# Yields, copy engines, mark times and list limit of a fused FFT and balanced-expert kernel

## The chip, the cores and the metric

The kernel runs on one core of one Trainium2 chip. The metric is the device time of one execution in microseconds (us). Before the change it is 576.92 us, the median of three runs (576.12 to 579.05).

The engines are named as in the profile: PE is TensorE's matmul, PEld its weight load, DVE is VectorE, ACT is ScalarE, POOL is GpSimd, and SP is the engine that issues plain DMAs.

## The reference

The input x has 8 batches of 2496 rows of 256 values. The reference takes the real part of the two-dimensional FFT of each batch, calls the 19968 resulting rows tokens, and gives every token to one of 8 experts, each of which takes exactly 2496 tokens. Then each token goes through its expert's two matrices.

```python
X = np.fft.fft(np.fft.fft(x, axis=1), axis=2).real          # 8 x 2496 x 256
logits = tokens @ w_gate                                    # 19968 x 8
for idx in np.argsort(-logits.flatten()):                   # best pair first
    tok, e = idx // 8, idx % 8
    if assigned[tok] >= 0 or counts[e] >= 2496: continue
    assigned[tok] = e; counts[e] += 1
out[mask_e] = np.maximum(tokens[mask_e] @ w1[e], 0) @ w2[e] # 256 -> 1024 -> 256
```

## The kernel before, in words

**Stages.** Loading, folding by symmetry and cosine/sine tables take the first 80 us or so. Then the logits are computed ahead of the transform. From about 100 us the transform runs in 20 parts (n = 0 to 19) of 1024 token places each. Each part has an even half and an odd half: ten matmuls each into one PSUM tile `fftps` (`even_half`, `odd_half`). ACT scales the even sum into `ev` (L1051) and casts the whole sum into `stage` (L1058). Then the part's *combination* (`combine` inside `odd_half`) writes the difference `ev - fftps` on DVE (L1061), negated columns on ACT (L1062) and mirrored columns on POOL (L1064, L1065), and SP stores 512 KB to `t_dram` (L1067). The combination on DVE is what frees the PSUM tile for a later even half: six of the eight parts that matter here rotate through three buffers "h", every fourth part has one buffer "t". Between the halves stand 16 pieces `wps` (L1104) that fold the feature transform into w1; their PSUM tile is the single buffer "o", which ACT copies out (L1030).

**The first chain.** Beside the transform a chain on DVE (`first_chain`: `choose`, `lowest`, `search`, `first_strips`) finds which tokens surely keep their first choice and gives each a place `spot` in a *strip*. It is a Python generator: a `yield` of some number of microseconds lets the loop `for c in first_chain()` (just before the sort loop) record that many microseconds' worth of transform halves, `unit()`, on the other engines' streams; a `yield SYNC` aligns the two estimated clocks. Every engine's stream is in the order in which it is recorded (a manual schedule), so a yield decides which combinations stand between two steps of the chain on DVE. In `first_strips` three additions of PSUM results (L884: experts 0-2 from a tile "o", 3-5 from "misc", 6-7 from "o" again) are followed by the tree of maxima `top_of` (L595 to L597), ten small operations up to `spot` (L902), the marks of part 0 (`sort_mark(0)`) and one yield of 7.0.

**The first sort.** A sort turns a part's 1024 token rows into rows grouped by expert. `sort_mark(n)` makes eight one-hot tiles `pt` on DVE (L1123, two buffers), `reload(n)` brings the part back from `t_dram` as `xl` (three buffers, L1132), `sort_call(n, gs)` multiplies the two on PE (L1145) and `take` copies PSUM to the strip `xs`. For strip 0 (parts 0 to 3) the PSUM tile alternates between the two single buffers "misc" and "o" (`side_ps`), and both are copied by ACT (L1030). `strip_places` (L911 to L917) and `payloads(0, ...)` (L584 to L589) prepare the row numbers, `sort_rows(0, 0)` (L1158 to L1162) and `sort_rows(0, 1)` (L1172 to L1179) make them; the matmuls of the latter write the PSUM buffer "t", which the combination of part 19 frees.

**The experts.** 40 strip tiles of 384 tokens come first (5 strips by 8 experts), then 16 late tiles: per expert one of 384 and one of LCAP - 384 places, which are gathered by an indirect DMA. Each tile has three parts: 3, 3 and 2 of its eight up products (L1282, ReLU copies by ACT L1030 or DVE L1034), each followed by one down product (L1305) of the tile before, whose 128 rows are copied and scattered to the output by an indirect DMA on POOL (L1309). A table `aside` puts other steps in front of a (tile, part): the marks, sorts and reloads of strips 1 to 4. After each part `pace` lets a second DVE chain, `settle_rest`, go on; it ends with the lists of late tokens (`decode`, L810 to L826), and only then can the gathers of late tiles (L1263, on POOL) be issued. A flag tells whether an expert has more late tokens than LCAP; if so, a slow fallback recomputes everything not placed.

Of the kernel before, what the change touches and what calls it, by code (L numbers as in the profile page):

```python
# [19 lines left out]
S = 2496  # L20
D = 256
# [23 lines left out]
TT = 384  # L45
SEG = 4096
LB = 6
LCAP = 736
SW = 24
NT = 5  # L50
GT = 16
EW = E * SW
# [18 lines left out]
def kernel(  # L71
# [437 lines left out]
    deep = {"ps": None, "sb": None, "n": 0}  # L509
# [84 lines left out]
    def top_of(dst, src):  # L594
        nc.vector.tensor_tensor(tree, src[:, 0:4, :], src[:, 4:8, :], op=AL.max)  # L595
        nc.vector.tensor_tensor(tree[:, 0:2, :], tree[:, 0:2, :], tree[:, 2:4, :], op=AL.max)
        nc.vector.tensor_tensor(dst, tree[:, 0, :], tree[:, 1, :], op=AL.max)  # L597
# [253 lines left out]
    def first_strips():  # L851
        low, wid, lo0 = found["low"], found["wid"], found["lo0"]
        lev = small("lev")
        nc.vector.scalar_tensor_tensor(lev, in0=wid, scalar=-0.01, in1=low, op0=AL.mult, op1=AL.add)
        moved = small("moved")
        nc.vector.tensor_tensor(moved, low, lo0, op=AL.is_gt)
        nc.vector.tensor_scalar(moved, in0=moved, scalar1=2.0 * T_FREE, scalar2=-T_FREE, op0=AL.mult, op1=AL.add)
        fits = small("fits")
        nc.vector.tensor_scalar(fits, in0=exc, scalar1=0.5, scalar2=2.0 * T_FREE, op0=AL.is_lt, op1=AL.mult)
        nc.vector.tensor_scalar(fits, in0=fits, scalar1=-T_FREE, scalar2=None, op0=AL.add)  # L860
        nc.vector.scalar_tensor_tensor(lev, in0=lev, scalar=moved, in1=fits, op0=AL.min, op1=AL.max)
        yield 0.8
        yield SYNC
        bps = misc()
        nc.tensor.transpose(bps[:, 0:P], lev.to_broadcast([P, P]), identf)
        thr = small("thr")
        nc.vector.tensor_reduce(thr, bps[:, 0:P], axis=AXX, op=AL.min)
        nc.vector.tensor_scalar(sure, in0=mx, scalar1=thr, scalar2=0.0, op0=AL.add, op1=AL.is_ge)
        nc.vector.scalar_tensor_tensor(sure, in0=mv, scalar=0.0, in1=sure, op0=AL.is_le, op1=AL.mult)
        nc.vector.scalar_tensor_tensor(ohb, in0=off, scalar=0.0, in1=sure[:, None, :].to_broadcast([P, E, GC]),  # L870
                                       op0=AL.is_le, op1=AL.mult)
        yield 2.3
        yield SYNC
        v = asg.tile([P, GC], FT, tag="sl_v", bufs=1, name="sl_v")
        for e0, ne in ((0, 3), (3, 3), (6, 2)):
            rps = (misc() if e0 == 3 else pso.tile([P, 512], FT, tag="o", bufs=1, name="rps"))[:, 0:ne * GC]
            rv, ov = (v_.rearrange("p (f k) -> p f k", k=NK) for v_ in
                      (rps, ohb[:, e0:e0 + ne, :].rearrange("p e c -> p (e c)")))
            nc.tensor.matmul(rv[:, :, 0:NK:2], lhsT=rankb, rhs=ov[:, :, 0:NK:2], start=True, stop=False)
            nc.tensor.matmul(rv[:, :, 1:NK:2], lhsT=rankf, rhs=ov[:, :, 1:NK:2], start=False, stop=False)  # L880
            nc.tensor.matmul(rps.rearrange("p (f s k) -> p f s k", s=2, k=NK)[:, :, 1, :], lhsT=onesb,
                             rhs=ohb[:, e0:e0 + ne, :].rearrange("p e (f s k) -> p (e f) s k", s=2, k=NK)[:, :, 0, :],
                             start=False, stop=True)
            nc.vector.tensor_tensor(wa[:, e0:e0 + ne, :].rearrange("p e c -> p (e c)"), rps,  # L884
                                    base[:, e0:e0 + ne, :].rearrange("p e c -> p (e c)"), op=AL.add)
        top_of(v, wa)
        v_i = asg.tile([P, GC], I32, tag="sl_vi", bufs=1, name="sl_vi")
        for cc in range(2):
            nc.vector.tensor_scalar(by_cols(v_i, cc), in0=by_cols(v, cc), scalar1=2.0 * SEG - (SW - SC[cc]) - MARK,
                                    scalar2=0.0, op0=AL.add, op1=AL.max)  # L890
        t1 = asg.tile([P, GC], I32, tag="sl_t1", bufs=1, name="sl_t1")
        t2 = asg.tile([P, GC], I32, tag="sl_t2", bufs=1, name="sl_t2")
        t3 = asg.tile([P, GC], I32, tag="sl_t3", bufs=1, name="sl_t3")
        nc.vector.tensor_scalar(t1, in0=v_i, scalar1=13, scalar2=None, op0=AL.arith_shift_right)
        nc.vector.tensor_scalar(t3, in0=v_i, scalar1=SEG - 1, scalar2=None, op0=AL.bitwise_and)
        has = asg.tile([P, GC], FT, name="has_e")
        for cc in range(2):
            hc, sc, vc, a1, a3 = (by_cols(t, cc) for t in (has, spot, v, t1, t3))
            nc.vector.scalar_tensor_tensor(hc, in0=a3, scalar=float(SC[cc]), in1=by_cols(sure, cc), op0=AL.is_lt,
                                           op1=AL.mult)  # L900
            nc.vector.scalar_tensor_tensor(vc, in0=a1, scalar=float(SC[cc]), in1=a3, op0=AL.mult, op1=AL.add)
            nc.vector.scalar_tensor_tensor(sc, in0=vc, scalar=1.0 - SC[cc], in1=hc, op0=AL.add, op1=AL.mult)  # L902
        early["has"] = has
        sort_mark(0)
        yield 7.0
        early["t"] = (v, t1, t2, t3)

    def strip_places():
# [114 lines left out]
    def take(dst, src, relu=False, eng=None):  # L1023
        n = 1
        for d in src.shape[1:]:
            n *= d
        ca, cd = 0.17 + n / 1280.0, 0.13 + n / 900.0
        if eng == "A" or eng is None and busy["A"] + ca <= busy["D"] + cd:
            busy["A"] += ca
            nc.scalar.activation(dst, src, ACT.Relu if relu else ACT.Copy)  # L1030
        else:
            busy["D"] += cd
            if relu:
                nc.vector.tensor_scalar(dst, in0=src, scalar1=0.0, scalar2=None, op0=AL.max)  # L1034
            else:
                nc.vector.tensor_copy(dst, src)  # L1036
# [81 lines left out]
    def sort_mark(n):  # L1118
        marks[n] = moe.tile([P, 8, EW + 2], BF, tag="pt", bufs=2, name="pt")
        b0, kc = NB * (n // NK), n % NK  # L1120
        for f in range(8):
            c, w = b0 * 4 * NK + f * NK + kc, E * SC[f % 2] + 1
            nc.vector.tensor_scalar(marks[n][:, f, 0:w], in0=rampw[:, 0:w], scalar1=spot[:, c:c + 1],  # L1123
                                    scalar2=None, op0=AL.is_equal)
        busy["D"] += 1.1
# [8 lines left out]
    def sort_call(n, gs, eng=None):  # L1134
        t, u = divmod(n, 4)
        if t not in strips:
            strips[t] = (deep["sb"] if t % 2 else moe).tile([P, 2, E, SW // 8, GT, 8], BF, tag="xs", bufs=1, name="xs")
        xl, pt = reloads[n], marks[n]
        dst = strips[t].rearrange("p j e c g i -> p (j e c) g i")
        for g in gs:  # L1140
            sps = side_ps("sps", eng)
            for cc in range(2):
                for j2 in range(2):
                    into = sps[:, j2 * EW:(j2 + 1) * EW].rearrange("p (e s) -> p e s", s=SW)
                    nc.tensor.matmul(into[:, :, SW - SC[cc]:], lhsT=xl[:, 2 * g + cc, j2 * P:(j2 + 1) * P],  # L1145
                                     rhs=pt[:, 2 * g + cc, 0:E * SC[cc]].rearrange("p (e s) -> p e s", s=SC[cc]), start=(cc == 0 and j2 == 0),
                                     stop=(cc == 1 and j2 == 1))
            take(dst[:, :, 4 * u + g, :], sps[:, 0:2 * EW].rearrange("p (m i) -> p m i", i=8), eng=eng)

    def sort_rows(t, part):  # L1150
        a_t = a8
# [47 lines left out]
    for c in first_chain():  # L1199
# [7 lines left out]
        clock["D"] = max(clock["D"], clock["PE"]) + 0.3  # L1207
        clock["PE"] = max(clock["D"], clock["PE"])
    for n in range(4):
        if n < 3:  # L1210
            sort_mark(n + 1)
        unit()
        sort_call(n, (0, 1), "A")
        unit()
        sort_call(n, (2, 3), "A")
        unit()
        reload(n + 3)
        if n == 0:
            strip_places()
        if n == 1:  # L1220
            payloads(0, payr)
    sort_rows(0, 0)
    while unit():
        pass
    flush()
# [121 lines left out]
    for t in range(1, NT):  # L1347
        for u in range(4):
            j, n = 8 * (t - 1) + 2 * u, 4 * t + u
            at(j, 0, lambda n=n: sort_mark(n))  # L1350
            at(j, 2, lambda n=n: sort_call(n, (0, 1)))
            at(j + 1, 1, lambda n=n: sort_call(n, (2, 3)))
            if n + 3 < 4 * NT:
                at(j + 1, 2, lambda n=n: reload(n + 3))
        at(8 * t - 4, 1, lambda t=t: sort_rows(t, 0))
        at(8 * t - 1, 0, lambda t=t: sort_rows(t, 1))
# [102 lines left out]
```

## Time and profile before

| | us |
|---|---|
| median of three runs | 576.92 |
| the profiled execution's own time | 526.67 |
| its span, first to last instruction | 524.8 |
| PE, PEld, DVE, ACT, POOL busy | 463.1, 349.5, 359.3, 331.9, 333.6 |

The profiled execution is 50.25 us faster than the median of the runs. Busy times are those of the span. In a timeline each row gives the start, the duration, the engine, the source line, the operation with its output and input tiles and the number of merged instructions; in brackets stands how long the engine sat idle before the row and what ended the wait. In a table of windows each row is a stretch of the span with the busy time of PE, PEld, DVE, ACT and POOL, then TensorE's granted clock as a share of full speed, the busy share of the DMA engines and what they moved in GB/s.

### The profile page before, as it was taken

Reading aid. Unit: us, or ns where it says so; the run is one execution under the profiler, and the core shown is the slowest. Engines: PE = TensorE matmul, PEld = TensorE weight load, DVE = VectorE, ACT = ScalarE, POOL = GpSimd, SP = SyncE. Lnnn points to the kernel's source line nnn. Section 1 sums busy time; section 2 is a strip of 40 time slices with the busy share of each in tenths; the row PEclk is TensorE's granted clock in tenths of the full one; section 3 lists DMA queues with packets and bytes.
Section 4 is the critical chain, followed back from the end, with each engine's and each line's share of the span. In section 5 each row is a group of like instructions: output and inputs, shape, how many; then the busy total and the mean of one; then the engine's idle time right before and its main releaser. Section 6 shows DMA issues by size and latency. Waiting matters only on the chain. (4 is left out here: it accounts for less than half of the span.)

```text
span 524.8 us, 11144 instructions
## 1 busy us (share of the span) xinstructions
PE 463.1 (88%) x3943; PEld 349.5 (67%) x3943; DVE 359.3 (68%) x930; ACT 331.9 (63%) x756; POOL 333.6 (64%) x381
## 2 busy tenths in 40 slices
PE   0657778898988999989989999999999999999991
PEld 0535546786766666767657877777777777777771
DVE  8799897385758989988998546666654555455450
ACT  7889884157567878777767676565655454545540
POOL 7888825295363556454533367777777777777774
PEclk9997889999997999999999999999999999999996
DMA  8999948259679797532322145552222224444421
GB/s 258 327 287 301 302 129 131 32 180 314 189 189 309 169 223 154 131 101 91 99 89 91 48 116 135 142 170 84 82 85 83 78 92 122 115 108 115 105 88 54
DMA packets 48482, 77.66 MB, mean 148 GB/s; under 512 B 19424, under 2 KB 27658, under 8 KB 48416
## 3 DMA queue, kind: packets, MB, share of 16 engines
q0 software_dynamic: 23296, 42.10, 31.5%
q1 hardware_dynamic: 25120, 34.75, 21.1%
q8 instruction: 33, 0.54, 0.4%
q14 instruction: 33, 0.27, 0.2%
HBM read 51.26 MB, written 32.24 MB: 159 GB/s over the span
## 5 line engine op out<-in xcount | busy, mean ns | idle before, releaser
L1030 ACT ACTIVATE hb<-hps 128x384 bf16<-128x384 f32 (+1 forms) x321 | 144.1, 492 | 56.5 <-PE hps L1282 52.7
L1305 PE MATMUL ops<-w2t,hb 128*128 128x256 bf16 (+1 forms) x1344 | 173.7, 273 | 0.0
L1305 PEld LDWEIGHTS <-hb 128*128 128x128 bf16 (+1 forms) x1344 | 132.3, 99 | 31.5
L1309 POOL DMA_INDIRECT out_dram<-zball,rid x83 | 88.8, 1070 | 74.6 <-ACT zball L1030 62.1
L1282 PE MATMUL hps<-xs,zball 128*128 128x384 bf16 x640 | 128.2, 329 | 0.1
L1282 PEld LDWEIGHTS <-zball 128*128 128x128 bf16 x896 | 85.9, 98 | 46.1 <-issue 8.2
L1034 DVE TENSOR_SCALAR hb<-hps 128x384 bf16<-128x384 f32 (+1 forms) x127 | 69.7, 549 | 52.3 <-PE hps L1282 36.9
L133 POOL DMA_INDIRECT xb<-in_x_dram,mir_i x40 | 54.9, 1372 | 11.9 <-issue 10.2
L1030 ACT ACTIVATE zball<-ops 128x256 f32<-128x256 f32 x85 | 32.7, 384 | 36.7 <-PE ops L1305 33.5
L1282 PE MATMUL hps<-xt,zball 128*128 128x384 bf16 (+1 forms) x256 | 47.7, 319 | 0.0
L289 PE MATMUL tp<-identf,xa 128*128 128x128 f32 x160 | 29.1, 350 | 17.2 <-ACT hi_cE L262 7.4
L289 PEld LDWEIGHTS tp<-identf,xa 128*128 128x128 f32 x160 | 25.0, 184 | 24.4 <-ACT hi_cE L262 7.8
L1030 ACT ACTIVATE xs<-sps 128x384 bf16<-128x384 f32 x60 | 27.4, 492 | 14.2 <-PE sps L1145 13.9
L1064 POOL COPY stage<-stage 128x258 bf16<-128x258 bf16 x40 | 17.6, 454 | 25.5 <-DVE stage L1061 16.6
L1145 PEld LDWEIGHTS <-xl 128*128 128x128 bf16 x320 | 25.9, 99 | 11.6 <-issue 8.7
L1123 DVE TENSOR_SCALAR pt<-rampw,spot 128x193 bf16<-128x193 bf16 (+1 forms) x160 | 32.2, 293 | 0.9 <-PE inv_ps L793 0.9
L1145 PE MATMUL sps<-pt,xl 128*128 128x192 bf16 (+1 forms) x288 | 27.7, 235 | 4.4 <-DVE pt L1123 3.5
L1263 POOL DMA_INDIRECT xg<-t_dram,ids_l x24 | 24.0, 1000 | 7.3 <-issue 7.0
L1309 POOL DMA_INDIRECT out_dram<-zball,rows_l x23 | 22.3, 968 | 7.0 <-issue 2.7
L1051 ACT ACTIVATE ev<-fftps 128x512 f32<-128x512 f32 x20 | 11.9, 600 | 19.3 <-DVE lg L496 9.2
L1309 POOL DMA_INDIRECT out_dram<-wa,rid x20 | 19.8, 988 | 6.1 <-issue 3.1
L1036 DVE COPY zball<-ops 128x256 f32<-128x256 f32 (+1 forms) x21 | 8.9, 425 | 21.3 <-PE ops L1305 14.3
(355 smaller groups left out, 771.9 us busy)
## 6 DMA issues: line engine op xcount, KB each, us to landing
t_dram<-stage SPq DMA_DIRECT2D x20, 512.0 KB
xl<-t_dram SPq DMA_DIRECT2D x20, 512.0 KB
xa<-in_x_dram SPq DMA_DIRECT2D x8, 1024.0 KB
w1raw<-in_moe_w_dram POOLq DMA_DIRECT2D x8, 512.0 KB
w2t<-in_moe_w_dram POOLq DMA_DIRECT2D x8, 512.0 KB
xa<-in_x_dram SPq DMA_DIRECT2D x8, 224.0 KB
out_dram<-zball,rid POOLq DMA_INDIRECT x83
xb<-in_x_dram,mir_i POOLq DMA_INDIRECT x40
```

The lines of the kernel that those rows point to most:

```text
L133: nc.gpsimd.indirect_dma_start(out=bv[0:n, i, :], out_offset=None, in_=x_pairs, in_offset=bass.IndirectOffsetOnAxis(ap=mir_i[0:n, b * NK + ...
L289: nc.tensor.transpose(tp[:, blk, u, :], pv[:, 4 * c + u, blk * P:(blk + 1) * P], identf)
L1030: nc.scalar.activation(dst, src, ACT.Relu if relu else ACT.Copy)
L1034: nc.vector.tensor_scalar(dst, in0=src, scalar1=0.0, scalar2=None, op0=AL.max)
L1051: nc.scalar.activation(ev, fps, ACT.Copy, bias=0.0, scale=2.0)
L1064: nc.gpsimd.tensor_copy(st[:, :, 1 + q, 0:P + 1], st[:, :, 3 * q, 0:P + 1])
L1123: nc.vector.tensor_scalar(marks[n][:, f, 0:w], in0=rampw[:, 0:w], scalar1=spot[:, c:c + 1], scalar2=None, op0=AL.is_equal)
L1145: nc.tensor.matmul(into[:, :, SW - SC[cc]:], lhsT=xl[:, 2 * g + cc, j2 * P:(j2 + 1) * P], rhs=pt[:, 2 * g + cc, 0:E * SC[cc]].rearrange("p ...
L1263: nc.gpsimd.indirect_dma_start(out=d["xg"][0:nr, q, :], out_offset=None, in_=t_dram, in_offset=bass.IndirectOffsetOnAxis(ap=d["ids"](q, nr ...
L1282: nc.tensor.matmul(hps[:, 0:n], lhsT=w1t[d["e"]][:, j2, fc * P:(fc + 1) * P], rhs=d["x"](j2), start=(j2 == 0), stop=(j2 == 1))
L1305: nc.tensor.matmul(ops[0:nr, 0:D], lhsT=d["hid"][:, fc, b0:b0 + nr], rhs=w2t[d["e"]][:, fc, :], start=(fc == 0), stop=(fc == F // P - 1))
L1309: put = nc.gpsimd.indirect_dma_start(out=out, out_offset=bass.IndirectOffsetOnAxis(ap=d["rows"](b0 // P)[0:nr], axis=0), in_=ot[0:nr, :], ...
```

## The change

The order of instructions on PE stays the same but for one group of three matmuls (the third addition's). On DVE the combinations, marks and part of the strip copies stand elsewhere. POOL's and SP's orders are the same, with shorter last pieces of late tiles.

- `LCAP` is 720 in place of 736: the second late tile of each expert has 336 places in place of 352.
- `first_strips` yields 1.3 after the second addition, 0.5 before and 1.7 after the tree of maxima, and 3.0 at the end (before: 7.0 at the end alone). `sort_mark(0)` is taken out of it.
- In `take`, an explicit "D" now means DVE; in `sort_call` of strip 0, tiles in "misc" are copied by DVE and tiles in "o" by ACT.
- In the first sort, `sort_mark(0)` and `strip_places` are done after one more unit, ahead of `sort_mark(1)`; `payloads` moves from after part 1 into part 0; `sort_rows(0, 0)` moves ahead of part 3.
- The marks of strips 1 to 4 are made at (j - 1, part 1) in place of (j, part 0), where their first sort is at (j, part 2): two parts earlier.

```diff
-LCAP = 736
+LCAP = 720
...
+            if e0 == 3:
+                yield 1.3
+        yield 0.5
         top_of(v, wa)
+        yield 1.7
...
         early["has"] = has
-        sort_mark(0)
-        yield 7.0
+        yield 3.0
...
-        if eng == "A" or eng is None and busy["A"] + ca <= busy["D"] + cd:
+        if eng != "D" and (eng == "A" or busy["A"] + ca <= busy["D"] + cd):
...
-            take(dst[:, :, 4 * u + g, :], sps[:, 0:2 * EW].rearrange("p (m i) -> p m i", i=8), eng=eng)
+            take(dst[:, :, 4 * u + g, :], sps[:, 0:2 * EW].rearrange("p (m i) -> p m i", i=8),
+                 eng=eng and ("D" if deep["side"] else "A"))
...
     for n in range(4):
+        if n == 0:
+            unit()
+            sort_mark(0)
+            strip_places()
         if n < 3:
             sort_mark(n + 1)
         unit()
-        sort_call(n, (0, 1), "A")
+        sort_call(n, (0, 1), "S")
         unit()
-        sort_call(n, (2, 3), "A")
+        if n == 0:
+            payloads(0, payr)
+        sort_call(n, (2, 3), "S")
         unit()
         reload(n + 3)
-        if n == 0:
-            strip_places()
-        if n == 1:
-            payloads(0, payr)
-    sort_rows(0, 0)
+        if n == 2:
+            sort_rows(0, 0)
...
-            at(j, 0, lambda n=n: sort_mark(n))
+            at(max(j - 1, 0), 1 if j else 0, lambda n=n: sort_mark(n))
```

In the changed order DVE's stream from the first addition on is: two additions, a combination, the third addition, the tree, a combination, the operations up to `spot`, two combinations, marks of part 0, `strip_places`, marks of part 1, a combination, a strip copy, `payloads`, a strip copy, a combination, marks of part 2, a copy, a combination, a copy, marks of part 3, two copies, `sort_rows(0, 0)`, two copies, the last combination. The third addition's matmuls stand on PE behind two more halves and two more pieces `wps`.

## The prediction

> **What bounds the kernel now.** I read the windows by stage first, then POOL's timeline to the end, then PE's and DVE's timelines in the stretch that the change rewrites. Columns of the windows: stretch, its length, busy time of PE, PEld, DVE, ACT, POOL with counts, TensorE's clock, DMA share, GB/s.
>
> ```profile
> 104.00:137.00 33.00, 31.64 (x272) 25.66 (x270) 22.89 (x57) 21.85 (x46) 25.00 (x45) 1.00 0.78 237
> 137.00:153.70 16.70, 14.78 (x114) 10.94 (x113) 12.33 (x37) 9.46 (x20) 8.32 (x17) 1.00 0.51 129
> 153.70:168.60 14.90, 11.65 (x137) 10.01 (x135) 9.99 (x35) 11.18 (x26) 5.75 (x11) 0.87 0.98 326
> 168.60:306.00 137.40, 130.90 (x1079) 93.96 (x1076) 117.03 (x367) 101.48 (x247) 65.51 (x61) 0.99 0.49 124
> 306.00:514.00 208.00, 207.11 (x1709) 159.29 (x1706) 112.38 (x267) 113.77 (x262) 158.91 (x162) 1.00 0.37 106
> ```
>
> PE is nearly always busy, but 137 to 168.6 (first sort) and 168.6 to 306 (experts beside the second chain) have holes of about 5 and 6.5 us. From 306 on PE looks full; POOL shows something else:
>
> ```profile
> 302.82 0.97 POOL L1309 DMA_INDIRECT out_dram<-zball,rid  x1 [2.37 <-ACT zball L1030]
> 305.08 0.97 POOL L1309 DMA_INDIRECT out_dram<-zball,rid  x1 [1.29 <-ACT zball L1030]
> 306.35 1.01 POOL L1263 DMA_INDIRECT xg<-t_dram,ids_l  x1 [0.30 <-DVE wa L826]
> ...
> 388.70 0.94 POOL L1263 DMA_INDIRECT xg<-t_dram,ids_l  x1 [0.30 <-issue]
> 389.94 0.99 POOL L1309 DMA_INDIRECT out_dram<-zball,rid  x1 [0.30 <-issue]
> ...
> 517.12 0.97 POOL L1309 DMA_INDIRECT out_dram<-zball,rows_l  x1 [0.30 <-ACTq L1407]
> 518.39 0.93 POOL L1309 DMA_INDIRECT out_dram<-zball,rows_l  x1 [0.31 <-issue]
> ```
>
> From 305.08 on no idle stretch exceeds 0.32 us: 166 indirect DMAs in 214.2 us, one per 1.29 us. PE's last product ends at 514.0, POOL's last issue at 519.3. So in this execution the end is the time at which the late lists are decoded (about 306) plus a full POOL queue. Before 306 POOL waits, and PE and DVE set the pace. In the first sort:
>
> ```profile
> 164.75 0.63 PE L1145 MATMUL misc<-pt,xl 128*128 128x192 bf16 x4 [0.94 <-DMA xl<-t_dram]
> 165.17 0.74 PE L1145 MATMUL sps<-pt,xl 128*128 128x192 bf16 x4
> 165.95 0.69 PE L1145 MATMUL misc<-pt,xl 128*128 128x192 bf16 x4
> 166.49 0.69 PE L1145 MATMUL sps<-pt,xl 128*128 128x192 bf16 x4
> 167.93 0.77 PE L1172 MATMUL rp<-bt,a 128*32 128x24 bf16 x32 [0.75 <-DVE stage L1061]
> ```
>
> ```profile
> 149.97 2.63 DVE L1123 TENSOR_SCALAR pt<-rampw,spot 128x193 bf16<-128x193 bf16 x8
> 152.51 0.68 DVE L1061 TENSOR_TENSOR stage<-ev,fftps 128x512 bf16<-128x512 f32 x1
> 157.60 0.69 DVE L1061 TENSOR_TENSOR stage<-ev,fftps 128x512 bf16<-128x512 f32 x1 [4.42 <-ACT stage L1058]
> ...
> 167.19 0.68 DVE L1061 TENSOR_TENSOR stage<-ev,fftps 128x512 bf16<-128x512 f32 x1
> ```
>
> Between 157.60 and 167.87 DVE never rests; its last combination releases the row-number matmuls at 167.93, and the experts start right behind, at 168.63. DVE, not ACT, ends this stage.
>
> [...] the windows show 0.50 from 164.9 to 171.7, [...]
>
> **Part by part.**
>
> *Earlier combinations.* PE's stall for a combination before 146.29 (0.97 us) goes: parts 12 and 13 are now freed before they are wanted. But the third addition's matmuls stand behind two more halves and two `wps` in the same PSUM buffer. From 139.0 (second addition's matmuls issued): even 1.11, `wps` 0.43, odd 1.11, then the second `wps` behind ACT's copy of the first, to 142.2; ACT's cast and copy end at 143.0, and the third group starts at 143.04, not 139.43. Its wait, 0.85 (the first group waited 0.69 in the same place), replaces 0.26. DVE adds at 143.6 in place of 139.96. Two late: PE gains 0.97 - 0.59 = 0.4 here, DVE sits idle from 140.6 to 143.6, 3.0 us.
>
> *Two engines for the copies.* Eight of 16 copies leave ACT (16 x 0.49 in the table of groups) and go to DVE, at 0.556 us (an `xs` copy of 128x384 on DVE; 0.55 apart when queued): 8 x 0.55 = +4.4 us of DVE. Freed PSUM waits on ACT were 0.55 us. Behind each copy on DVE stand combinations and marks for PE, and behind those, PE's next sort.
>
> *Moves in the sort.* `strip_places` 2.55 (158.21 to 160.75), `payloads` 1.0, `sort_rows(0,0)` 1.9, marks 1.4 a part: moved, not changed. No DMA moves past another on SP or POOL.
>
> *Sum for DVE to the last combination.* DVE had from 138.72 to 167.19 idle stretches of 0.91 + 0.94 + 4.42 = 6.3 us. New: 4.4 of copies and 3.0 of waiting = 7.4. Laid out: add 3 143.6, tree to 145.8, combination 146.4, `spot` 148.4, two combinations 149.7, marks 151.0, places 153.6, marks 155.0, combination 155.6, copy 156.1. PE reaches the second sort pair at 155.5 and waits 0.65 for that copy, so its 0.4 us are gone. Then payloads 157.1, copy 157.65, combination 158.25, marks 159.65, copy 160.2, combination 160.8, copy 161.5, marks 162.9, copy 163.45; PE starts the next pair at 163.5 (before 162.98), copy 164.5, `sort_rows` 166.4, copy 166.95, PE's last pair 167.0, copy 167.95, combination 168.55, row-number matmuls 168.6, experts 169.3. Before: 168.63. **+0.7 us.** DVE's 6.3 us of cover are gone, so from here every further microsecond on DVE counts. POOL's copies of two combinations now fall on the marks of part 0 (149 to 152): between 0 and 1.2 us (2.63 - 1.46), **I take +0.6**. The reload that made PE wait 0.94 at 164.75 no longer shows. The half clock costs about half of 6.8 us less the idle part, 2.8 us, today; [...] it may not come at all (-2.8): **+0.2**.
>
> *Marks two parts earlier.* Three PE waits for marks are 2.00 (at 234.25), 0.60 (278.23) and 0.87 (308.95). They go. But between 227 and 278 the second chain on DVE rules: PE waits for it again at 262.77 (0.42), 265.90 (0.54), 266.69 (0.52) and 273.75 (0.82). From the threshold at 227.07 to the flag at 273.53 the chain held three sets of marks, and in the new order it holds three again (one moves out in front, delaying the start by 0.5; one moves in, right in front of the flag). So PE's 2.0 us turn into waits at these points, and after 278 PE stands where it stood. Decoding waits for PE (2.58 us), which hides the mark that now stands before it. The 0.87 lies behind POOL's full queue. **0**, bounds -2.6 (the first two waits) and +0.9.
>
> *LCAP.* Eight gathers and eight scatters have 80 rows in place of 96. POOL's 96-row DMAs take 0.94, those of 128 rows 0.99, so 16 rows are 0.025 us: 16 x 0.025 = **-0.4 us** on the path. PE saves 128 products x 16 columns; 352 columns take 0.15 us a product and 384 0.163 (rows of six, start to start), so 0.0067 x 128 = 0.85 us, hidden by POOL's queue; it counts instead of the 0.4 where PE is late. From the reference's inputs the largest late list comes out at 698, so 720 holds.
>
> *Sum:* 0.7 + 0.6 + 0.2 + 0 - 0.4 = +1.1 us. The profiled execution, 526.67 (span 524.8 and 1.9 around it), would become 527.8. The runs' median lies 50.25 us higher; no view says why, so I carry the difference over unchanged: 576.92 + 1.1 = **578.0**.
>
> **Rivals.**
> 1. *The sort stage is mended.* The waits 0.97, 0.55, 0.19 and 0.94 go (2.65), the clock never drops (2.8), and in the runs PE rather than POOL is late, so LCAP gives 0.85 and the 0.87 counts. For it: DVE's contention and copies may overlap better than my serial list. Against: DVE had no rest from 157.6. Sum -7.2: 569.7. Half of it, 573.3, is its near edge.
> 2. *DVE becomes the bound of the first sort, in earnest* (slower). It decides once DVE has over 1.5 us more work than in my list by 168: the whole 1.2 of contention in place of 0.6 (+0.6), one more half-clock window (+1.7 in place of +0.2), and the flag 0.9 late: 1.1 + 0.6 + 1.5 + 0.9 = +4.1: 581.0.
> 3. *The list overflows* and the fallback runs: eight experts x seven tiles at 5.3 us (118 scatters, three a tile, in the 208 us after 306) are some 300 us more. Against: 698 of 720.
>
> **Chances.** My forecast 0.60 (574.0 to 579.8), rival 1 0.12, rival 2 0.27, rival 3 0.01. The measurement tells about 0.5% from no change, 2.9 us; my case lies within it, so faster 0.12, same 0.60, slower 0.28. The range leaves out rival 3, the far half of rival 1 and the tail of rival 2: 573.0 to 582.5.
>
> **What would show it.** The first product of the experts near 170 in place of 168.63; DVE without idle from 144 to 169; the third group on PE near 143; no PE wait for marks after 200, but longer ones for the flag; POOL unbroken from about 307. I am wrong if the experts start before 168, if the clock stays full through 165 to 172, or if the flag's product does not come later relative to the experts' start.

## The result, and the profile after

| | before | after |
|---|---|---|
| median of the runs, us | 577.75 (4 runs) | 583.59 (582.46 to 585.0, 4 runs) |
| ratio, 95% interval | | 1.0104 (1.0066 to 1.0141) |
| profiled execution, its span | 526.67, 524.8 | 583.18, 581.2 |
| PE, PEld, DVE, ACT, POOL busy | 463.1, 349.5, 359.3, 331.9, 333.6 | 473.8, 351.5, 359.8, 324.5, 330.3 |

The changed kernel is 1% slower; the forecast of 578.0 (573.0 to 582.5) was wrong. The two profiled executions can't be compared as wholes: in the one before PE ran without pauses after 306 (busy 207.11 of 208.00 us), in the one after it had them (220.88 of 262.00), and sessions (sets of runs taken together) differ in this whatever the kernel: the kernel before took 577.75, 578.36 and 581.36 us in three of them and 524.51 and 524.11 in two. Each ratio below therefore compares a kernel with the kernel before in its own session. The windows of the profile after, cut at the same events (first sort, first expert product, first gather):

```profile
137.00:153.70 16.70, 14.96 (x117) 11.16 (x115) 11.63 (x34) 10.37 (x22) 8.06 (x15) 1.00 0.68 213
153.70:170.70 17.00, 11.41 (x132) 9.70 (x131) 14.86 (x47) 7.47 (x16) 6.33 (x12) 0.85 0.76 231
170.70:308.00 137.30, 130.62 (x1082) 94.95 (x1079) 117.86 (x376) 101.80 (x249) 64.44 (x62) 0.98 0.50 121
308.00:570.00 262.00, 220.88 (x1705) 162.72 (x1703) 107.56 (x258) 108.77 (x260) 158.91 (x162) 0.97 0.28 84
```

The second row is the place: the end of the first sort lasts 17.0 us (before 14.9), DVE is busy 14.86 of them (before 9.99 of 14.9) and ACT 7.47 (before 11.18). The third row has the old length, 137.3 to 137.4. In PE's timeline, after:

```profile
156.62 0.44 PE L1148 MATMUL misc<-pt,xl 128*128 128x192 bf16 x4 [0.97 <-DVE xs L1039]
...
164.65 0.44 PE L1148 MATMUL misc<-pt,xl 128*128 128x192 bf16 x4 [1.49 <-DVE xs L1039]
...
168.13 0.69 PE L1148 MATMUL misc<-pt,xl 128*128 128x192 bf16 x4 [0.98 <-DVE xs L1039]
...
170.06 0.77 PE L1176 MATMUL rp<-bt,a 128*32 128x24 bf16 x32 [0.71 <-DVE stage L1064]
170.76 4.02 PE L1289 MATMUL hps<-xs,zball 128*128 128x384 bf16 x12
```

PE's waits are now for the strip copies on DVE (`xs`), which free the buffer "misc", and the experts start at 170.76 in place of 168.63. DVE's timeline says why the copies are late:

```profile
143.50 0.49 DVE L884 TENSOR_TENSOR wa<-rps,base 128x320 f32<-128x320 f32 x1 [3.03 <-PE rps L881]
...
158.26 2.59 DVE L1126 TENSOR_SCALAR pt<-rampw,spot 128x193 bf16<-128x193 bf16 x8
160.76 0.54 DVE L1039 CAST xs<-misc 128x384 bf16<-128x384 f32 x1
...
162.31 1.83 DVE L1126 TENSOR_SCALAR pt<-rampw,spot 128x193 bf16<-128x193 bf16 x8
164.06 0.54 DVE L1039 CAST xs<-misc 128x384 bf16<-128x384 f32 x1
...
169.33 0.68 DVE L1064 TENSOR_TENSOR stage<-ev,fftps 128x512 bf16<-128x512 f32 x1
```

Copies stand behind groups of marks, and two of these groups take 2.59 and 1.83 us, not the 1.4 of the forecast.

### The profile page after: what moved, and what is told of

Its sections match the earlier page's. It is cut to its first block, busy times and chain, and to the rows that moved or that the text cites. A ratio compares the mean times of both kernels' runs of the same rounds, so it can differ in the third digit from the quotient of the medians.

```text
span 581.2 us, 11130 instructions
## 1 busy us (share of the span) xinstructions
PE 473.8 (82%) x3943; PEld 351.5 (60%) x3943; DVE 359.8 (62%) x938; ACT 324.5 (56%) x748; POOL 330.3 (57%) x381
## 4 chain that ended last, share of the span: by engine, by line
PE 59%; DVE 13%; issue 9%; ACT 9%; POOL 3%; another core or an unknown queue 2%; DMA 2%; SPq 0%; POOLq 0%; ACTq 0%; DVEq 0%
PE hps L1289 25%; PE ops L1312 22%; PE tp L289 3%; PE sps L1148 3%; DVE pt L1126 2%; DMA t_dram<-stage 2%; ACT zt L291 2%; PE yps L299 1%; ACT zball L1033 1%; ACT tf L258 1%; DVE hb L1037 1%; PE wps L1107 1%; ACT hb L1033 1%; PE fftps L453 1%
## 5 line engine op out<-in xcount | busy, mean ns | idle before, releaser
L1033 ACT ACTIVATE hb<-hps 128x384 bf16<-128x384 f32 (+1 forms) x320 | 141.3, 492 | 81.2 <-PE hps L1289 58.8
L1312 PE MATMUL ops<-w2t,hb 128*128 128x256 bf16 (+1 forms) x1344 | 177.8, 276 | 0.5 <-issue 0.5
L1312 PEld LDWEIGHTS <-hb 128*128 128x128 bf16 (+1 forms) x1344 | 134.0, 100 | 34.8 <-issue 2.4
L1289 PE MATMUL hps<-xs,zball 128*128 128x384 bf16 x640 | 133.9, 334 | 20.0 <-issue 7.8
L1289 PE MATMUL hps<-xt,zball 128*128 128x384 bf16 (+1 forms) x256 | 50.4, 320 | 15.3 <-ACT hb L1033 6.1
L133 POOL DMA_INDIRECT xb<-in_x_dram,mir_i x40 | 53.6, 1339 | 14.0 <-issue 10.2
L289 PE MATMUL tp<-identf,xa 128*128 128x128 f32 x160 | 26.8, 330 | 20.7 <-issue 10.4
L289 PEld LDWEIGHTS tp<-identf,xa 128*128 128x128 f32 x160 | 22.7, 171 | 28.1 <-issue 12.8
L1148 PEld LDWEIGHTS <-xl 128*128 128x128 bf16 x320 | 27.7, 104 | 12.7 <-issue 10.1
L1067 POOL COPY stage<-stage 128x258 bf16<-128x258 bf16 x40 | 17.8, 458 | 25.8 <-DVE stage L1064 19.9
L1148 PE MATMUL sps<-pt,xl 128*128 128x192 bf16 (+1 forms) x288 | 29.3, 243 | 3.9 <-DVE hb L1037 3.0
L348 DVE TENSOR_TENSOR xa<-xa,xb 128x2550 f32<-128x2550 f32 (+2 forms) x10 | 22.8, 2282 | 0.0
```

What stands on the lines that cost most here:

```text
L133: nc.gpsimd.indirect_dma_start(out=bv[0:n, i, :], out_offset=None, in_=x_pairs, in_offset=bass.IndirectOffsetOnAxis(ap=mir_i[0:n, b * NK + ...
L289: nc.tensor.transpose(tp[:, blk, u, :], pv[:, 4 * c + u, blk * P:(blk + 1) * P], identf)
L348: nc.vector.tensor_tensor(a_t[:, i0:i1, :, 1:D], a_t[:, i0:i1, :, 1:D], b_t[:, i0:i1, ::-1, D - 1:0:-1], op=AL.add)
L1067: nc.gpsimd.tensor_copy(st[:, :, 1 + q, 0:P + 1], st[:, :, 3 * q, 0:P + 1])
L1289: nc.tensor.matmul(hps[:, 0:n], lhsT=w1t[d["e"]][:, j2, fc * P:(fc + 1) * P], rhs=d["x"](j2), start=(j2 == 0), stop=(j2 == 1))
L1312: nc.tensor.matmul(ops[0:nr, 0:D], lhsT=d["hid"][:, fc, b0:b0 + nr], rhs=w2t[d["e"]][:, fc, :], start=(fc == 0), stop=(fc == F // P - 1))
```

## The experiments

Three stretches are read from each kernel's timelines: the *stage* from the first ranking matmul (`rps`, L879) to the first expert product, the *middle* to the first gather, and the *late* part to POOL's last instruction. All three are lengths in us of one profiled execution. What lies ahead of the stage is the same code in all and took 135.6 to 139.3 us. "Before there" is the median of the kernel before in the same session, and the ratio is to it.

| kernel | before there | ratio (95%) | stage | middle | late |
|---|---|---|---|---|---|
| before, first profile | | | 30.59 | 137.73 | 212.97 |
| after, first profile | 577.75 | 1.0104 (1.0066, 1.0141) | 32.79 | 137.24 | 267.00 |
| e1_before | 578.36 | 1.0008 (0.9984, 1.0032) | 30.05 | 137.74 | 264.48 |
| e2_lcap736 | 578.36 | 1.0084 (1.0051, 1.0117) | 33.14 | 138.51 | 262.43 |
| e3_marks_back | 578.36 | 1.0056 (1.0034, 1.0078) | 32.80 | 138.11 | 264.76 |
| e4_sort_back | 578.36 | 1.0001 (0.9973, 1.0029) | 30.08 | 138.11 | 263.99 |
| e5_after | 524.51 | 1.0061 (1.0037, 1.0084) | 32.87 | 138.08 | 213.34 |
| e6_copies_act | 524.51 | 1.0010 (0.9991, 1.0029) | 31.46 | 138.11 | 213.32 |
| e7_yields_back | 524.51 | 1.0083 (1.0060, 1.0106) | 32.85 | 138.08 | 213.14 |
| e8_order_back | 524.51 | 1.0082 (1.0056, 1.0107) | 33.64 | 137.14 | 213.35 |
| e9_copies_only | 524.11 | 1.0125 (1.0085, 1.0164) | 34.97 | 138.44 | 212.91 |
| e10_pool_to_act | 524.11 | 1.0080 (1.0055, 1.0104) | 36.24 | 137.21 | 213.14 |
| e11_yields_only | 524.11 | 1.0021 (0.9996, 1.0046) | 30.54 | 137.77 | 212.91 |
| e12_order_only | 524.11 | 0.9970 (0.9952, 0.9989) | 28.60 | 137.65 | 212.90 |
| e13_time_only | 581.36 | 1.0067 (1.0044, 1.0090) | 32.25 | 137.79 | 269.52 |
| e14_wait_only | 581.36 | 1.0054 (1.0031, 1.0077) | 32.32 | 137.98 | 267.50 |
| e15_order_720_marks | 581.36 | 1.0017 (0.9991, 1.0042) | 28.42 | 136.53 | 268.54 |

### Which of the three parts loses

**e1_before**: the kernel before, no edit.

> The kernel before, unchanged, for a second profile of it. Its first profiled execution took 526.67 us while its timed runs took 576 to 579; the profiled execution of the changed kernel took 583.18, like its timed runs. If the 50 us are a way of running that an execution can fall into (the late phase with PE pausing), this one should show 575 to 580 with a span of 574 to 578, PE idle some 50 us more after 306 than the 0.9 us of the first profile, and POOL no longer issuing back to back. If the first profile was typical and the timed runs carry something outside the span, its span will be near 525 again. The experts should start near 168.6 in both cases.

The span was 575.3 us and the late part 264.48 us in place of 212.97. The windows, of this kernel and then of the changed one in a session without pauses (e5_after):

```profile
306.00:566.00 260.00, 220.98 (x1697) 162.66 (x1695) 107.19 (x261) 108.28 (x258) 158.92 (x162) 0.96 0.28 85
```

```profile
309.30:515.00 205.70, 205.70 (x1706) 159.05 (x1703) 109.66 (x258) 112.19 (x260) 157.54 (x159) 1.00 0.36 106
```

The work is the same, but PE is idle for 39 us in the first (I expected some 50) and busy 15 us longer; in the second it is never idle. The 50 us are a way of running, not a trait of either kernel.

**e2_lcap736**, the changed kernel with

```diff
-LCAP = 720
+LCAP = 736
```

> The changed kernel with the late limit back at 736. Theory A (the loss was made in the first sort, 2.1 us of it seen as experts that start at 170.76 in place of 168.63): the limit is worth -0.4 to -0.9, so this run takes 584 to 585. Theory B (the loss is in the late phase: 80-row pieces or 336-column products cost more than the 96-row and 352-column ones): this run takes 579.5 to 581.

The ratio was 1.0084 and the stage 33.14. The median, 582.62 us, lies between the bands of the two theories, but the kernel is still slower than before, so the limit isn't the loss.

**e3_marks_back**, the changed kernel with

```diff
-            at(max(j - 1, 0), 1 if j else 0, lambda n=n: sort_mark(n))
+            at(j, 0, lambda n=n: sort_mark(n))
```

> The changed kernel with the marks at their old place in the experts. My prediction's step: nothing, 583 to 584, and three PE waits for marks (2.0, 0.6, 0.9) come back while the flag's product comes no later. Theory C (the marks put before the chain of the second choice make it, and all after it, later): 580 to 582, and the first gather earlier than 307.99. If the early marks gain what they were meant to: 585 to 587.

The ratio was 1.0056, close to the changed kernel's 1.0061 in e5 below. The median, 581.14 us, falls into theory C's band, but the first gather came at 309.93, not earlier than 307.99, and the middle lasted 138.11. The early marks neither gain nor lose anything that can be seen.

**e4_sort_back**: the kernel before with the reverse of these two edits.

> The kernel before with the limit 720 and the early marks, so the changed kernel without its first sort (no new yields, all sort copies on ACT, sort steps in their old order). Theory A (DVE became the bound of the first sort): experts start at 168.6 again and the time is 577 to 579, at most 581.5 if only the 2.1 us of the start are given back. Theories B or C (the limit, or the marks): 582 to 584, the experts' start notwithstanding.

The ratio was 1.0001 and the stage 30.08, as theory A said: the loss is made in the first sort. **e5_after**, the changed kernel again, gave the size without the pauses:

> The changed kernel once more, beside the three that follow. The stage from the first ranking matmul of the slot chain to the first expert product took 32.79 us in its first profile, 30.05 and 30.08 in the profiles of the two kernels with the old first sort. If the whole loss is these 2.7 us, this run takes 581 against some 578.4 of the kernel before; if it is 584 again, some 2.5 to 3 us more are lost behind the first sort.

The ratio was 1.0061, which is 3.2 us (1.9 to 4.4). Of these the stage has 2.3 against the first profile of the kernel before and 2.8 against e1 and e4.

### Which part of the first sort

**e6_copies_act**, the changed kernel with

```diff
-                 eng=eng and ("D" if deep["side"] else "A"))
+                 eng=eng)
-        sort_call(n, (0, 1), "S")
+        sort_call(n, (0, 1), "A")
```

and the same for (2, 3).

> The changed kernel with all sort copies on ACT again. Theory A1 (the eight copies on DVE, 8 x 0.55, stand behind marks that PE does not need yet, and hold PE's one PSUM buffer): the stage shrinks from 32.8 to 30 to 30.7 and the time is 578 to 580. Theory A2 (the third addition that comes 3 us late starts DVE late): the stage stays above 32 and the time at 581 to 584, for DVE has as little rest before 169 as now. Theory A3 (the order of the marks, places and row numbers): as A2.

The ratio was 1.0010: with the copies goes the loss that can be measured. The stage, though, is 31.46, not 30 to 30.7, and 1.4 shorter than with the copies (32.87). In PE's timeline:

```profile
163.84 0.71 PE L1148 MATMUL misc<-pt,xl 128*128 128x192 bf16 x4 [3.21 <-DMA xl<-t_dram]
```

DVE was done early here, and PE waited for the fourth part's reload instead. POOL's timeline tells what held this reload up:

```profile
153.77 0.41 POOL L1067 COPY stage<-stage 128x258 bf16<-128x258 bf16 x1 [3.68 <-DVE stage L1064]
...
154.94 0.76 POOL L338 DMA_DIRECT2D w1raw<-in_moe_w_dram  x1
```

The combination that stands on DVE behind `strip_places` and two groups of marks comes late. POOL's copies wait for it, and behind them the last 512 KB load of `w1raw` on POOL; on SP a store of 512 KB waits, and behind it the reload. Load, store and reload are all issued between 19.4 and 19.9 us into the stage. From 151.6 to 154.9 the DMA engines have almost nothing to do (busy share 0.08); from 155.4 on, while the reload is on its way, they are full (0.97). In e12 below the load goes out 15.2 us into the stage, the DMA engines are full in the same 3.3 us of the stage (1.03), and PE doesn't wait for the reload. In e5 the late reload shows too: PE waits 1.28 us for it before 167.13. That the bunching alone makes the reload late is read from these traces, no run tested it.

**e7_yields_back** and **e8_order_back**, the changed kernel with the old yields of `first_strips` (marks of part 0 back at its end), and with the old order of the loop:

```diff
-            if e0 == 3:
-                yield 1.3
-        yield 0.5
         top_of(v, wa)
-        yield 1.7
```

```diff
+        if n == 0:
+            strip_places()
+        if n == 1:
+            payloads(0, payr)
+    sort_rows(0, 0)
```

> The changed kernel with the slot chain's old yields and the first part's marks at its end again; copies on two engines and the loop's other order stay. Theory A1: DVE gains the 3.0 us of waiting for the third addition, so that its list has room for the copies again: the stage is 31 to 32, the time 580 to 582. Theory A2: the stage is 30 to 30.7, the time 578 to 579.5. Theory A3: 32 or more, 582 to 584.

> The changed kernel with the old order of the first sort's loop (places behind the first part, payloads behind the second, row numbers behind the fourth, one half less ahead of the first part); the slot chain's yields and the copies on two engines stay. Theory A3: the stage is 30 to 30.7, the time 578 to 579.5. Theories A1 and A2: the stage stays at 32 to 33.5 and the time at 581.5 to 585, for the row numbers then stand behind the last marks, right before the row-number matmuls.

The ratios were 1.0083 and 1.0082, the stages 32.85 and 33.64: taking back either of the two alone doesn't take back the loss. In e7 all groups of marks took 1.47 to 1.60 us, but `strip_places` began 15.0 us into the stage, in the changed kernel 13.8: the loss is there without stretched marks, in a list that starts later. Nor is it TensorE's clock: in e7 it was half only in the last 0.8 us of the stage (the last four products of the sort took 0.44, the row-number matmuls at 168.14 took 0.77), as in e4, whose stage was 30.08.

**e9_copies_only**, the kernel before with the diff of `take` and `sort_call` alone, the reverse of e6. (The line changed in `take` has no effect of its own: an explicit "D" went to DVE before it too.)

> The kernel before with nothing but the copies on two engines. If the eight copies on DVE are enough for the loss (the stage was 32.8 to 33.6 in the three kernels that had them, 31.5 without): stage 31.5 to 33, 0.3 to 0.8% slower than before. If the copies only hurt together with the new order or the late third addition: stage 30 to 30.7, no difference; DVE had 4.42 us of rest ahead of 157.60 which the first two copies can use.

The ratio was 1.0125, the highest of all and more than I expected: the copies alone cost 6.6 us (4.5 to 8.6), of which the stage has 4.4 to 4.9, and the whole change cost 3.2 in e5. PE's timeline:

```profile
164.42 0.44 PE L1145 MATMUL misc<-pt,xl 128*128 128x192 bf16 x4 [1.98 <-DVE xs L1036]
...
170.70 0.77 PE L1173 MATMUL rp<-bt,a 128*32 128x24 bf16 x32 [2.63 <-DVE stage L1061]
```

**e11_yields_only** and **e12_order_only**, the kernel before with one of the other two parts (in e12 the marks of part 0 leave the chain and the loop is the new one, all copies "A"; in e11 the last yield is 4.4).

> The kernel before with nothing but the slot chain's yields (the combinations between its additions, the third addition late; the first marks stay at the chain's end, 7.9 us of yields in all). Step 'earlier combinations' of my prediction: PE gains 0.4 and DVE loses 3.0 us that its later rest (4.42) covers, so the stage is 29.5 to 30.3 and the time within 0.2% of before. If the late third addition alone costs: stage 31 and more, over 0.2% slower.

> The kernel before with nothing but the new order of the first sort's loop (copies on ACT, old yields). The run with the copies back on ACT had a stage of 31.46, with PE waiting 3.21 us for the fourth part's reload. If the order makes that (places and the second marks, 4 us, ahead of a combination whose store the reload waits for): a wait for the reload of 2 to 3.5 us before the last sort pair, stage 31 to 31.7, 0 to 0.25% slower. If not: stage 30 to 30.4 and the usual 0.9 to 1.3 us of wait.

The yields alone gave a stage of 30.54 and 1.0021, which isn't told from no change. The order alone gave a stage of 28.60 and 0.9970 (0.9952 to 0.9989): it is faster, where I expected it to be no faster. PE's timeline of e12 at the end of the stage:

```profile
163.28 0.44 PE L1144 MATMUL misc<-pt,xl 128*128 128x192 bf16 x4 [0.18 <-ACT xs L1029]
163.67 0.44 PE L1144 MATMUL sps<-pt,xl 128*128 128x192 bf16 x4
164.44 0.71 PE L1171 MATMUL rp<-bt,a 128*32 128x24 bf16 x32 [0.33 <-DVE stage L1060]
```

The waits of before for the reload (0.94) and the last combination (0.75) have shrunk to 0.33, and TensorE's clock stays full (the row-number matmuls take 0.71 us, 0.77 in the kernel before at half clock).

The parts don't add up. e6 and e15 (below) differ in the yields alone, and their stages are 31.46 and 28.42: yields that cost nothing on the kernel before cost 3.0 us beside the new order, where they hold up the loads as e6 shows. The copies cost 4.4 to 4.9 us of the stage on the kernel before, 4.3 beside the new order (e12, e7) and 1.4 in the changed kernel (e6, e5), where PE would otherwise wait for the reload. e15 and e12 ran in other sessions than e6 and e7.

### Why the copies cost so much

**e10_pool_to_act**, the changed kernel with POOL's share of the combination on ACT for five parts (the old lines follow under an `else`):

```diff
+            if 14 <= n <= 18:
+                for q in range(2):
+                    nc.scalar.copy(st[:, :, 1 + q, 0:P + 1], st[:, :, 3 * q, 0:P + 1])
+                nc.scalar.activation(st[:, :, 2, P + 1:D], st[:, :, 3, P + 1:D], ACT.Copy, bias=0.0, scale=-1.0)
...
```

> The changed kernel with POOL's three copies of the combinations of halves 14 to 18 on ACT (15 x 0.41 us more there, where ACT is busy 7.3 of 16.3 us). If POOL's copies are what stretched the marks (2.09, 2.65 and 1.83 in place of 1.4 to 1.5) and DVE is the bound: the three groups of marks take 1.3 to 1.5 each, the stage falls from 32.9 to 30.7 to 31.5, and the time is 0 to 0.4% above before. If the marks shrink and the stage stays above 32.3, DVE's length was not what PE waited for; if the marks don't shrink, POOL was not what stretched them.

DVE's timeline, the marks of parts 0 to 2:

```profile
149.99 1.47 DVE L1131 TENSOR_SCALAR pt<-rampw,spot 128x193 bf16<-128x193 bf16 x8
153.31 1.46 DVE L1131 TENSOR_SCALAR pt<-rampw,spot 128x193 bf16<-128x193 bf16 x8
160.35 1.47 DVE L1131 TENSOR_SCALAR pt<-rampw,spot 128x193 bf16<-128x193 bf16 x8
```

POOL's copies are what stretched the marks (2.09, 1.46 and 2.59 in the changed kernel). But stretched marks alone don't make the loss: in e6 they took 2.10, 1.47, 2.52 and 1.97. For the time e10 is inconclusive: ACT became late, PE waited 2.15 and 1.50 us for its copies of `wps`, and the stage grew to 36.24.

**e13_time_only** and **e14_wait_only** are e12 with something added in `sort_call` where the copy stood on DVE; nothing uses what it makes (`lf` and `wf` are flat views of `lg` and `wa`):

```diff
+            if eng is not None and deep["side"]:
+                nc.vector.tensor_tensor(wf[:, 0:384], lf[:, 0:384], lf[:, 384:768], op=AL.add)      # e13
+                nc.vector.tensor_copy(small("peek"), sps[:, 0:1])                                   # e14
```

> The kernel with the new order only (stage 28.6, 0.3% faster than before), with eight additions on DVE from SBUF to SBUF of about 0.55 us each put where the copies stood in DVE's queue; the copies stay on ACT. They compute nothing that is used. Theory 'time' (DVE's 4.4 us more in a stage whose end DVE sets): stage 31.5 to 33, 0.3 to 0.8% slower than before. Theory 'coupling': DVE had 5.5 us of rest in the stage and takes the time from it, stage 28.6 to 30, no slower than before.

> The kernel with the new order only, with a read of one column (128x1) of each of the eight sort tiles by DVE at the place where its copy stood; ACT still copies. They compute nothing that is used. DVE now waits for PE, and PE's buffer for DVE, for some 0.1 us of work each. Theory 'coupling': stage 31 to 33, 0.3 to 0.8% slower than before. Theory 'time': stage 28.6 to 29.6, 0.1 to 0.4% faster than before.

> The kernel with the new order only, with the limit 720 and the early marks added. By the runs so far both are worth nothing (1.0001 with the old first sort): 0.2 to 0.5% faster than before, like the order alone (0.997). If the early marks or the limit cost something behind an earlier start of the experts: 0 to 0.2% faster.

Both theories hold: either addition makes the stage 32.3, against 28.42 of e15 in the same session, and the copies themselves make it 32.85 (e7). PE's timeline of e13:

```profile
165.05 0.44 PE L1144 MATMUL sps<-pt,xl 128*128 128x192 bf16 x4
169.52 0.77 PE L1174 MATMUL rp<-bt,a 128*32 128x24 bf16 x32 [4.03 <-DVE stage L1060]
```

PE sorts nearly undisturbed, ends as early in the stage as in e12, and waits 4.03 us for the end of DVE's list: eight additions of about 0.55 us, unhidden. DVE rested 5.5 us in e12's stage, but 4.5 of them (0.90, 1.19 and 2.40) before the marks of part 0, in front of all added work. The last two:

```profile
146.69 0.69 DVE L1060 TENSOR_TENSOR stage<-ev,fftps 128x512 bf16<-128x512 f32 x1 [1.19 <-ACT stage L1057]
149.78 0.69 DVE L1060 TENSOR_TENSOR stage<-ev,fftps 128x512 bf16<-128x512 f32 x1 [2.40 <-ACT stage L1057]
```

In e14 it is the other way round, on PE and then on DVE:

```profile
168.44 0.69 PE L1144 MATMUL misc<-pt,xl 128*128 128x192 bf16 x4 [1.27 <-DVE s_peek L1149]
...
170.51 0.77 PE L1173 MATMUL rp<-bt,a 128*32 128x24 bf16 x32 [0.85 <-DVE stage L1060]
```

```profile
168.23 0.15 DVE L1149 COPY s_peek<-misc 128x1 f32<-128x1 f32 x1
169.69 0.16 DVE L1149 COPY s_peek<-misc 128x1 f32<-128x1 f32 x1 [1.31 <-ACT xs L1029]
169.77 0.69 DVE L1060 TENSOR_TENSOR stage<-ev,fftps 128x512 bf16<-128x512 f32 x1
```

Eight reads of 0.15 us lengthen the stage by 3.9 us: PE waits for a read that stands behind marks and row numbers on DVE, DVE then rests (1.31) until the next tile is made and ACT has copied it, and the last combination stands behind that. In the profile each read starts only after ACT's copy of the same tile (0.49), so copy and read together hold the buffer, and e14 isn't the waiting on DVE alone. Why the two costs, 3.8 and 3.9, don't add up in the real copies is not tested; it would fit that the copy's time passes while the other side waits.

e15 (order, limit, early marks) had the shortest stage, 28.42, and yet 1.0017 (0.9991 to 1.0042), where I expected it 0.2 to 0.5% faster. It isn't told from no change, and its interval doesn't meet that of e12. Whether the limit and the marks take the gain back, or the session's pauses hide it, stays open. The one version that was measured faster than the kernel before is e12, in one session.

## Why the prediction was wrong, point by point

- **POOL's queue sets the end.** This fits where PE has no pauses: the late part is 212.90 to 213.35 us in all nine profiles of that kind. In the session of the result and in two others it doesn't, and the late part is 262 to 270 us long. Carrying the 50.25 us over unchanged was no explanation. It moved the level rightly only because the session of the result had the pauses, and it hid that another bound held.
- **Earlier combinations.** Right: the third addition's matmuls came at 142.98 (forecast 143.04), DVE waited 3.03 us (3.0), and the yields alone changed the stage by nothing (30.54). What they do beside the new order (e6) was not in the forecast.
- **DVE's list, the step that failed.** It stood at 158.26 at the marks of part 2 (forecast 158.25): the marks of part 0 had been 0.7 longer, places, payloads and copies as much shorter. The marks of part 2 then took 2.59 in place of 1.4, those of part 3 1.83, and the experts came at 170.76, where list and additions (169.3 + 0.6 + 0.2) said 170.1. The bound was the right one, a term of it was mis-sized: "I take +0.6" for POOL beside the marks. I charged one group, and three were stretched, by 0.62, 1.12 and 0.36 against 1.47, some 2.1 us in all. The list had also set the four groups at 1.3 to 1.4 each, 5.5 us, while the kernel before spent 7.21 on them (1.47, 2.63, 1.46, 1.65); the changed one spends 7.97. In the kernel before, the group at 149.97 took 2.63 us while POOL copied without a pause (148.23 to 154.41), and the groups at 144.18 and 160.75, with no copy of POOL beside them, 1.47 and 1.46; in e10, without POOL's copies, the marks of parts 0 to 2 took 1.46 to 1.47. The stretch was in my text (2.63 - 1.46); I didn't go through the list for every place where a copy of POOL falls on marks. That the changed kernel would be faster without the stretch no run shows.
- **"Moved, not changed"** was about durations. Row numbers took 1.92 as forecast, places and payloads less (2.24 and 0.72), marks more. What the order is worth by itself the forecast didn't ask: alone it shortened the stage by 1.5 to 2.0. In e12 `strip_places` runs from 15.6 to 17.8 us into the stage, where DVE rested in the kernel before (15.2 to 19.6). The +0.7 for the whole list held this gain and the price of the copies (4.3 beside the new order) in one number.
- **"No DMA moves past another"** is true and not enough: store, load and reload are issued later and bunched. The reload that was to show no longer kept PE waiting for 1.28 us in e5, 0.74 in e2 and 1.43 in e3. Their stages, 32.80 to 33.14, are about as long as that of the first profile after (32.79), where it doesn't show, so DVE's list and not the reload seems to set the end there.
- **The clock.** In the profile after it was half (0.50) from 165.5 on for 10.2 us, in the first profile of before from 164.9 on for 6.8: 3.4 longer, as the second rival had it (+1.7). In e5 it was half for 6.8 (four of the sort's products took 0.44 us up to 165.41, 0.71 from 167.13 on). What halves the clock, and what ends it, no run shows; the forecast's +0.2 for it was my estimate. I compared with one execution that ran at half clock for 6.8 us; two other profiles of the old sort (e1 and e4) had 3.4 us of it there and stages of 30.05 and 30.08, 0.5 us shorter. That the clock makes these 0.5 us isn't shown: e11's stage had no half clock and lasted 30.54.
- **Marks two parts earlier: 0.** Right in sum: e3 and e4, and middles of 136.5 to 138.5 either way. The mechanism came true as well: PE's waits for marks (2.00, 0.60) are gone, and new ones stand before the chain's products, 1.59 for `lists_x` and 2.23 in place of 0.82 for the flag. But the flag's product was to come later after the experts' start, and did so by 0.3 in the profile after (105.4 against 105.1), while in e4 and e5 it came 0.5 earlier (104.6).
- **LCAP: -0.4.** Wrong in sign. The late part is 213.14 to 213.35 with 720 and 212.90 to 212.97 with 736. A gather of 80 rows mostly takes 0.92 to 0.93 us, one of 96 rows 0.93 to 0.95: 16 x 0.01 = 0.16, not 0.4. And the first 80-row gather took 1.57 to 1.59 us in e5, e6, e7, e8 and e10, all the profiles with 720 and no pauses; why is open.
- **Sum.** +1.1, and 0.7 (experts at 170.76, not 170.1), 0.5 (the stage of the execution compared with) and 0.75 (limit) more, make 3.05; e5 measured 3.2 (1.9 to 4.4). This account was made after the fact, from single profiles. The result's first measurement, 5.8 to 6.0, is larger; its interval (3.8 to 8.1) overlaps, and the rest of it stays unexplained.
- **The rival that came true** is the second, DVE as the bound of the first sort. Its point of decision, 1.5 us of DVE more than in the list, was just about reached: the last combination ended at 170.01, in the list at 168.55. Of its three additions the contention came, the further half clock came in the profile after (10.2 us against 6.8) and not in e5 (6.8), and the flag 0.9 later didn't come.

## What to carry to other kernels

Before handing work to an engine because it rests in a stage, see *when* it rests: rest that lies ahead of the new work hides none of it, and e13 paid 3.8 us for 4.4 us of "free" time. In this kernel a read of a single PSUM buffer was better on the engine with less standing before it in its queue: at the places of the copies even reads of one column lengthened the stage by 3.9 us. Ask also which transfers an instruction releases: a combination that is late on DVE held up a load, a store and a reload. And when a change has several parts, run each alone and then pairs of them: here a part that gained 0.3% was hidden by one that lost 1.25%, and yields that cost nothing alone cost 3.0 us of the stage beside the new order.

## What the runs showed of the hardware that was not expected

Whole sessions differed by over 50 us for the same kernel, with PE pausing up to 3.0 us at a time in the profile after, but only after about 306 (from 250 to 306 it is busy 52.49 us, in the profile before 52.83). The chip's number doesn't tell the two apart: e1 to e4 and e9 to e12 are both recorded on chip 10, the former with the pauses and the latter without; whether it was the same machine isn't on record. In e1_before's waits of that part PE's weight loads stood 39.1 us in all for nothing that the profile shows. The traces of the sessions with pauses hold 5291 to 5478 semaphore updates, those without 8645 to 8777; the profile after has 5308 of them for 11130 instructions, the one before 8771 for 11144, so in the former a good part of the records seems to be missing. In the profile after PE's updates arrive bunched after a pause (six between 325.67 and 325.93 us, after none for 3.0 us). What makes PE pause no run here shows; the cause stays open.
